# Pooled attention into a snake MLP on one core: k of the first batch summed and turned by TensorE, its rest and half of the next k elsewhere

## The chip, the cores and the metric

The kernel runs on one core of a Trainium2 chip. The metric is the device time of one execution in microseconds; a number of executions gives a median. A profile of one execution shows each engine's instructions: TensorE (PE, with its weight loads as PEld), VectorE (DVE), ScalarE (ACT), GpSimd (POOL) and SyncE (SP), which issues most transfers.

## What is computed

q, k and v have 8 batches, 8 heads, 576 tokens and 64 channels, all float32.

```python
k_p = k.reshape(B, H, Sp, 8, D).mean(axis=3)      # 72 pooled keys
v_p = v.reshape(B, H, Sp, 8, D).mean(axis=3)
attn = softmax(scale * q @ k_p.T)                 # (q x 72) for each head
x = (attn @ v_p), heads side by side              # 4608 x 512
h = x @ w_in                                      # 512 -> 2048
g = h + sin(alpha * h)**2 / alpha
out = g @ w_out                                   # 2048 -> 512
```

## The kernel before

The large products use Strassen's scheme with seven products for eight. One loop, `hidden(u, extra)`, makes h and g for 512 tokens at a time (nine times, `NU`), in 28 slots: slot 7J + k makes product k of group J, in the order 1, 5, 6, 2, 7, 3, 4, and each product is four matmuls of 128x128 by 128x256 on line 734. The attention of the next batch is threaded into these slots. `carry(u)` lists, slot by slot, what else is emitted there: `at(slot, function, arguments)`. Every engine executes its instructions strictly in the order of emission, so this list is the order of each queue: that of SP, which issues transfers, as well as those of the computing engines. An instruction waits only for the data and buffers that it needs, but all behind it on its engine waits too. The results go through a bridge in HBM (`store_g`, `load_g`) to `outputs()`, which makes the last product (line 1034).

Batch 0 has no earlier loop to hide in: `first_batch()` writes its order out by hand. Its q is loaded two heads at a time with four tokens in a row (`load_q_heads`); the last 64 tokens of each head are "rest" (`load_q_rest`, kept in a part of the w_in buffer `A[3]` that is not in use yet). Its v lies in rows of four tokens too (`load_v_rows`), and TensorE adds the rows: in `sum_v_rows` a constant matrix `twos` (128 rows, 64 columns, ones where a column's two rows meet) is one operand and each of the four tokens the other; `eights` (64 rows, a column for 8 rows) does the same for the rest. Its k is loaded two heads at a time by `load_k_twice` into 72 partitions, one for each pooled key, eight tokens in a row; VectorE (pairs 0 and 1) or GpSimd (pairs 2 and 3) adds them in three steps (lines 146 and 148), the last of which writes the sum twice, side by side. `k_head(hp)` has TensorE transpose this (line 337), and ScalarE copies the result into `kb2`, so that each head's pooled k stands in both halves of the partitions. Then for each pair of heads `hp`: `q_head` transposes q (line 348), `products_head` multiplies (line 369), `soft_head` subtracts the maximum (VectorE, lines 375 and 377) and takes the exponential (ScalarE, 379), `norm_head` divides by the sum (lines 385 to 391), `a_head` transposes (419, 425), and `values` multiplies by v (506, 508) and writes x into a "home" buffer. `warm(n, i)` issues n matmuls of the identity matrix whose result nothing reads (line 830).

Batch 1 (the second) comes next: `load_k(1, e)` loads half of its heads (e = 0 or 1) into a "kvin" buffer on 96 partitions, of which there are two, and `pool_rows` has GpSimd add the tokens in three steps (line 117). `k_t` in slot 4 transposes the sums. `pairs_q` reorders its q on ScalarE, `q_t` transposes q, `two_scores` multiplies, `exp` and `norm` (GpSimd, line 328) follow, `turn` transposes 32x32 blocks on VectorE, `move` issues 16 transfers (line 462), and `all_values` in slot 25 multiplies by v (535, 548). `load_v(1, ...)` uses a kvin buffer again and has GpSimd add.

`load_w_in_part(J)` loads the part of w_in for group J, in four transfers; `combine_w_in(J, steps)` makes Strassen's sums of it (line 605) on VectorE or GpSimd. `sums_of_x(u, n)` makes those of x on VectorE (line 707). `score(4)` and `rest_q` treat the rest of q of batch 0. `root()` computes constants from alpha.

Of the kernel before, what the change touches and what calls it, by code (L numbers as in the profile page):

```python
# [14 lines left out]
AX = mybir.AxisListType.X  # L15
AF = mybir.ActivationFunctionType
OP = mybir.AluOpType
PSUM = bass.MemoryType.PSUM

P = 128  # L20
POOL = 8
# [19 lines left out]
class Kernel:  # L41
# [58 lines left out]
        return (qm[:, 0:n].rearrange("p (h t d) -> p h t d", h=self.H, t=4),  # L100
                qm[:64, n:].rearrange("p (h d) -> p h d", h=self.H))

    def load_k(self, b, e):

        Sp, D, NP = self.Sp, self.D, self.NP
        m = Sp // 3
        t = self.kvp.tile([P, 2048], F32, name="kvin")[:NP * m, 0:3 * POOL * D]
        self.nc.sync.dma_start(out=t, in_=self.k[b, NP * e:NP * e + NP].rearrange("h (p x) d -> (h p) (x d)", x=3 * POOL))
        if b not in self.kp:
            self.kp[b] = self.ap.tile([NP * m, 3, 2, D], F32, name="kp")  # L110
        self.pool_rows(t.rearrange("p (j x) -> p j x", j=3), self.kp[b][:, :, e, :])

    def pool_rows(self, t, out):

# [23 lines left out]
        nc.gpsimd.tensor_tensor(out=vz[:], in0=x[:, 0:D].unsqueeze(1).to_broadcast([P, H // 2, D]),  # L138
                                in1=self.mask[:].unsqueeze(2).to_broadcast([P, H // 2, D]), op=OP.mult)

    def load_k_twice(self, i, eng, t):

        Sp, D = self.Sp, self.D
        self.nc.sync.dma_start(out=t, in_=self.k[0, 2 * i:2 * i + 2].rearrange("h (p t) d -> p h (t d)", t=POOL))
        for w in (4 * D, 2 * D):
            eng.tensor_tensor(out=t[:, :, 0:w], in0=t[:, :, 0:w], in1=t[:, :, w:2 * w], op=OP.add)
        both = lambda x: x.unsqueeze(2).to_broadcast([Sp, 2, 2, D])
        eng.tensor_tensor(out=self.k2[:, 2 * i:2 * i + 2], in0=both(t[:, :, 0:D]), in1=both(t[:, :, D:2 * D]), op=OP.add)

    def load_v_rows(self, b, main, rest):  # L150

# [61 lines left out]
    def attention(self, b):  # L213

        nc, D, H, Sp, NP, S = self.nc, self.D, self.H, self.Sp, self.NP, self.S
# [114 lines left out]
        def new_a():  # L330
            self.aM = self.ap.tile([P, 4, 736], F32, name="aM")

        def k_head(hp):

            ps = self.psum([P, 2, Sp], 7 if hp % 2 else 0)
            for e in range(2):
                nc.tensor.transpose(ps[:, e, :], self.k2[:, 2 * hp + e].rearrange("p u d -> p (u d)"), self.ident[:Sp, :Sp])
            nc.scalar.copy(out=self.kb2[:, 2 * hp:2 * hp + 2], in_=ps)

        def q_head(hp):  # L340
# [184 lines left out]
        def all_values():  # L525
# [24 lines left out]
            for hp in hps:  # L550
                to_x(ps[hp].rearrange("p (t j) -> p j t", t=4), hp, 0, 512)
            to_x(rest, slice(0, 4), 512, 64)

        return SimpleNamespace(**{f.__name__: f for f in (k_t, q_t, products, score, two_scores, two_shifts, exp, norm, new_a, turn, move, values, values_rest, all_values,
                                                          k_head, q_head, rest_q, products_head, soft_head, norm_head, norm_rest, a_head, a_rest)})

# [260 lines left out]
    def first_batch(self):  # L819

        nc = self.nc
        self.att = [self.attention(b) for b in range(self.B)]
        A = self.att[0]

        far = [self.home(i, [P, 2, 2, POOL * self.D]) for i in (1, 2)]
        h = [self.hp.tile([P, 4 * POOL * self.D], F32, name="h") for _ in range(2)]
        self.load_alpha(self.hp.tile([P, P], F32, name="s", bufs=1)[:])
        one = self.sm.tile([P, 1], F32, name="one")
        nc.scalar.activation(out=one[:], in_=self.ident[:, 0:1], func=AF.Exp)
        warm = lambda n, i: [nc.tensor.matmul(self.psum([P, P], i), self.ident[:], self.ident[:], start=True, stop=True) for _ in range(n)]  # L830
        warm(3, 3)
        self.turn_alpha()
        tr = self.new_tr()
        nc.gpsimd.memset(tr[:, 2048:], 0.0)
        self.a0 = tr[:, 0:2048].rearrange("p (t j s k) -> p t j s k", t=4, j=4, s=2)
        self.z0 = tr[:, 2048:2560].rearrange("p (t hp x k) -> p t hp x k", t=4, hp=4, x=4)
        n, m = self.H * self.Sp, 2 * self.DM
        self.kb2 = h[1][:, 0:n].rearrange("p (h k) -> p h k", h=self.H)
        self.k2 = h[1][:self.Sp, n:n + m].rearrange("p (h u d) -> p h u d", h=self.H, u=2)
        self.a4 = self.last[:64, 0:512].rearrange("p (j s k) -> p j s k", j=4, s=2)  # L840
        self.z4 = self.last[:64, 512:640].rearrange("p (hp x k) -> p hp x k", hp=4, x=4)
        nc.gpsimd.memset(self.z4, 0.0)
        self.new_q(0)
        for hp in range(4):
            self.load_k_twice(hp, nc.vector if hp < 2 else nc.gpsimd, far[hp // 2][:self.Sp, hp % 2])
            self.load_q_heads(0, 2 * hp, 2 * hp + 2)
        self.load_v_rows(0, h[0][:], self.tp.tile([P, self.DM], F32, name="p5")[:])
        self.load_w_in()
        self.load_w_in_part(0)
        self.q_rest = self.A[3][:64, 0, 512:1024].rearrange("p (h d) -> p h d", h=self.H)  # L850
        A.new_a()
        warm(4, 3)
        A.q_head(0)
        warm(2, 4)
        A.k_head(0)
        for hp in range(4):
            A.products_head(hp)
            if hp < 3:
                warm(2, 1 + (hp + 1) % 2)
                A.q_head(hp + 1)  # L860
                A.k_head(hp + 1)
            A.soft_head(hp)
            if hp == 3:
                self.sum_v_rest(0, 0)
            if hp:
                A.norm_head(hp - 1, nc.vector if hp == 1 else nc.gpsimd)
        self.load_q_rest(0, self.q_rest)
        self.load_q(1)
        for e in range(2):
            self.load_k(1, e)  # L870
        self.load_w_in_part(1)
        A.norm_head(3, nc.vector)
        self.sum_v_rows(0, 0, 2)
        A.a_head(0, (1, 7, 0))
        self.sum_v_rows(0, 1, 2)
        A.values((0, 1), (4, 1))
        self.combine_w_in(0, (0, 1))
        A.a_head(1, (5, 6, 2))
        self.combine_w_in(0, (2, 3), nc.gpsimd)
        self.root()  # L880
        self.sums_of_x(0, 0)

    def carry(self, u):

        x = defaultdict(list)
        at = lambda slot, f, *a: x[slot].append(lambda: f(*a))
        last = self.B - 1
        b = u + 1
        if u == 0:
            A0, A = self.att[:2]  # L890
            at(1, A0.values, (2, 3), (2, 7))
            at(1, self.sums_of_x, 0, 1)
            at(1, self.sums_of_x, 0, 2)
            at(1, self.sums_of_x, 0, 3)
            at(2, self.load_w_in_part, 2)
            at(2, self.load_w_in_part, 3)
            at(2, A0.rest_q)
            at(3, A0.score, 4)
            at(2, self.pairs_q, 1, range(5))
            at(4, self.combine_w_in, 1, (0, 1, 2, 3), self.nc.gpsimd)  # L900
            at(4, A.q_t, 0, self.nc.vector.tensor_copy)
            at(4, A.q_t, 1, self.nc.vector.tensor_copy)
            at(4, A.k_t)
            at(7, self.load_v, 1, 0)
            at(7, self.load_v, 1, 1)
            for i in range(2):
                at((5, 10)[i], A.two_scores, i)
            at(11, A.two_shifts)
            for i in range(2, 5):
                at(5 + i, A.q_t, i)  # L910
            at(9, A0.exp, 4)
            for i in range(4):
                at((9, 9, 15, 15)[i], A.exp, i)
                at((10, 10, 16, 16)[i], A.norm, i)
                at((13, 13, 17, 17)[i], A.turn, i)
            at(8, self.combine_w_in, 2, (0, 1, 2, 3), self.nc.gpsimd)
            at(10, self.combine_w_in, 3, (0, 1, 2, 3), self.nc.gpsimd)
            at(20, A0.norm_rest)
            at(23, A0.a_rest)
            at(24, lambda: A0.values_rest((5, 6, 7, (self.turn + 1) % 5)))  # L920
            for r in (32, 96):
                at(3, self.nc.gpsimd.memset, self.aM[r:r + 32, :, 704:736], 0.0)
            at(17, A.move, 0)
            at(17, A.move, 1)
            at(25, A.all_values)
            at(9, self.load_q, 2)
            at(14, self.load_q, 3)
            for e in range(2):
                at(16, self.load_k, 2, e)
            at(26, self.att[2].k_t)  # L930
            turn = 23
        else:
            at(0, self.sums_of_x, u, 2)
            at(0, self.sums_of_x, u, 3)
        if 0 < u < last:
            A = self.att[b]
# [341 lines left out]
```

## Time and profile before

| | us |
|---|---|
| five runs, median | 925.91 |
| lowest, highest | 922.28, 928.20 |
| the profiled execution, its time | 927.38 |
| the profiled execution, its span | 925.5 |

The span is the time from the first to the last recorded instruction; what lies around it is 1.9 us. A line of the timeline gives the start, the busy time, the engine, the line of the kernel, the operation, and output <- input with partitions x elements; "x32" is the number of instruction records in it, and "[0.37 <-ACT h L338]" is the idle time of the engine ahead of it and what ended it. TensorE's records count a float32 product twice (a `products_head` of 16 matmuls is x32), a transpose once. In a list of waits the columns are: who waited for whom, the total, the number of times, the longest, all in us. In a table by stretch each row gives from:to, the length, then busy us and instructions of PE, PEld, DVE, ACT and POOL, the granted TensorE clock, the busy share of the 16 transfer engines and what they moved in GB/s.

### The profile page before, as it was taken

What the parts mean: (1) busy time and instruction counts of PE and PEld (TensorE: products, weight loads), DVE (VectorE), ACT (ScalarE), POOL (GpSimd) and SP (SyncE); (2) the same over time, 40 slices, a digit from 0 to 9 for tenths busy, and PEclk for the clock granted to TensorE, in tenths of its full rate; (3) what the DMA queues carried; (4) which work ended last, traced back from release to release, by engine and by line L of the source; (5) the groups of instructions that cost most, each with busy time, mean ns of one, the idle gap of its engine ahead of it and who ended that gap; (6) DMA issues with size and microseconds to landing.
All of it is one profiled execution on the core that took longest, in us unless ns stands there. A gap on an engine that the chain in (4) does not pass through costs nothing.

```text
span 925.5 us, 17725 instructions
## 1 busy us (share of the span) xinstructions
PE 903.8 (98%) x7009; PEld 818.0 (88%) x7009; DVE 668.6 (72%) x1007; ACT 436.7 (47%) x995; POOL 163.7 (18%) x155
## 2 busy tenths in 40 slices
PE   7998999999999999999999999999999999999997
PEld 6686888887888888888888899999999999999997
DVE  7665666745657466673466989988888888988894
ACT  4595686864867658676786631111111211112111
POOL 4684250522505225040000000000000000000000
PEclk9999999999999999999999999999999999999999
DMA  9975756766557646636526237161526353433401
GB/s 240 240 220 166 191 154 182 219 177 185 150 175 229 180 131 173 173 118 217 199 92 226 87 120 226 32 222 36 188 69 171 87 167 91 148 110 114 144 14 39
DMA packets 134130, 141.12 MB, mean 152 GB/s; under 512 B 49808, under 2 KB 102048, under 8 KB 134048
## 3 DMA queue, kind: packets, MB, share of 16 engines
q1 hardware_dynamic: 132976, 138.81, 52.0%
q10 hardware_dynamic: 1072, 1.19, 0.4%
q8 instruction: 55, 0.90, 0.4%
q14 instruction: 27, 0.22, 0.1%
HBM read 75.37 MB, written 47.19 MB: 132 GB/s over the span
## 4 chain that ended last, share of the span: by engine, by line
PE 86%; DMA 5%; DVE 2%; POOL 2%; SPq 2%; ACT 1%; issue 1%; POOLq 0%; DVEq 0%; ACTq 0%
PE PS L1034 41%; PE PS L734 40%; PE PS L271 2%; PE PS L535 2%; DMA kvin<-in_v_dram 1%; DMA q<-in_q_dram 1%; DVE sm L326 1%; DMA a<-in_moe_w_in_dram 1%; PE PS L548 1%; POOL as L605 1%; SPq L462 1%; SPq L599 1%; DVE h L713 1%; DMA home<-in_k_dram 1%; POOL ex L328 1%
## 5 line engine op out<-in xcount | busy, mean ns | idle before, releaser
L734 PE MATMUL PS<-home,a 128*128 128x256 f32 x1152 | 266.0, 382 | 5.1 <-DVE h L713 4.2
L734 PEld LDWEIGHTS PS<-home,a 128*128 128x128 f32 x1152 | 216.6, 190 | 44.2 <-DVE h L713 7.5
L734 PE MATMUL PS<-home,as 128*128 128x256 f32 x864 | 201.1, 382 | 1.0 <-DVE home L707 1.0
L734 PEld LDWEIGHTS PS<-home,as 128*128 128x128 f32 x864 | 163.2, 191 | 24.4 <-DVE home L707 2.0
L1034 PE MATMUL PS<-s,wb 128*128 128x144 f32 x896 | 119.3, 286 | 0.4 <-ACT PS L1147 0.4
L1034 PEld LDWEIGHTS PS<-s,wb 128*128 128x128 f32 x896 | 113.7, 190 | 0.7 <-ACT PS L1147 0.6
L713 DVE TENSOR_TENSOR h<-PS,p 128x512 f32<-128x512 f32 x72 | 49.1, 684 | 89.3 <-PE PS L734 55.8
L747 ACT ACTIVATE s<-s,c 128x256 f32<-128x256 f32 (+1 forms) x216 | 110.0, 572 | 0.0
L117 POOL TENSOR_TENSOR kvin<-kvin 96x768 f32<-96x768 f32 (+3 forms) x42 | 70.0, 1667 | 203.5 <-DMA kvin<-in_v_dram 185.2
L740 ACT ACTIVATE s<-h,al 128x256 f32<-128x256 f32 x144 | 65.1, 500 | 63.0 <-DVE h L713 62.1
L1147 ACT COPY PS<-PS 128x144 f32<-128x144 f32 x56 | 14.7, 263 | 146.0 <-PE PS L1034 144.6
L740 ACT ACTIVATE s<-PS,al 128x256 f32<-128x256 f32 x144 | 60.1, 468 | 29.6 <-PE PS L734 21.2
L1034 PE MATMUL PS<-r,wb 128*128 128x144 f32 x512 | 73.2, 286 | 0.0
L1034 PE MATMUL PS<-s,a 128*128 128x144 f32 x512 | 73.2, 286 | 0.0
L801 DVE TENSOR_TENSOR h<-PS,s 128x512 f32<-128x512 f32 x36 | 24.7, 685 | 60.1 <-ACT s L747 60.1
L1034 PEld LDWEIGHTS PS<-r,wb 128*128 128x128 f32 x512 | 67.1, 190 | 0.1
L1034 PEld LDWEIGHTS PS<-s,a 128*128 128x128 f32 x512 | 67.0, 190 | 0.0
L1166 ACT COPY PS<-PS 128x144 f32<-128x144 f32 x56 | 14.7, 263 | 88.2 <-PE PS L1034 88.2
L1034 PE MATMUL PS<-s,we 128*128 128x144 f32 x384 | 54.9, 286 | 0.0
L1034 PE MATMUL PS<-x,wb 128*128 128x144 f32 x384 | 54.9, 286 | 0.0
L1034 PEld LDWEIGHTS PS<-s,we 128*128 128x128 f32 x384 | 50.4, 190 | 0.1
L1034 PEld LDWEIGHTS PS<-x,wb 128*128 128x128 f32 x384 | 50.3, 190 | 0.0
(178 smaller groups left out, 1188.5 us busy)
## 6 DMA issues: line engine op xcount, KB each, us to landing
g_bridge<-h SPq DMA_DIRECT2D x72, 512.0 KB
r<-g_bridge SPq DMA_DIRECT2D x31, 1152.0 KB
out_dram<-o SPq DMA_DIRECT2D x128, 72.0 KB
kvin<-in_k_dram SPq DMA_DIRECT2D x14, 576.0 KB
q<-in_q_dram SPq DMA_DIRECT2D x7, 1024.0 KB
kvin<-in_v_dram SPq DMA_DIRECT2D x14, 512.0 KB
aM<-tr SPq DMA_DIRECT2D x56, 92.0 KB
aM<-tr SPq DMA_DIRECT2D x56, 88.0 KB
```

Source lines behind the costliest of these rows:

```text
L117: self.nc.gpsimd.tensor_tensor(out=t[..., 0:w] if w > D else out, in0=t[..., 0:w], in1=t[..., w:2 * w], op=OP.add)
L271: nc.tensor.matmul(ps[e][r0 + r:r0 + r + q.shape[-1], h, :], q[s], kb[s, hp, :], start=True, stop=True)
L326: nc.vector.tensor_reduce(out=sm, in_=E(i, Sp + 1), axis=AX, op=OP.add)
L535: nc.tensor.matmul(o[r:r + 64], w, x, start=start and i < 2, stop=False, skip_group_check=True)
L713: add = lambda o, x, y: nc.vector.tensor_tensor(out=o, in0=x, in1=y, op=OP.add)
L734: nc.tensor.matmul(ps[:, jj, :], self.A[p][:, kk, f * P:(f + 1) * P], x[:, kk, :], start=(start and jj == 0 and kk == 0), stop=(kk == 1), ...
L740: nc.scalar.activation(out=G.s[:, i, jj, j, :], in_=src[:, jj], func=AF.Sin, scale=self.al[:, f:f + 1])
L747: nc.scalar.activation(out=x, in_=x, func=AF.Square, scale=self.c[:, f:f + 1])
L801: add = lambda o, x, y: self.nc.vector.tensor_tensor(out=o, in0=x, in1=y, op=OP.add)
L1034: nc.tensor.matmul(out, W[:, J // 2, J % 2, :], A[:, J, :], start=(start and J == 0), stop=(J == self.NJ - 1), skip_group_check=True)
L1147: nc.scalar.copy(out=x1[:, 0, :], in_=x0[:, 1, :])
L1166: nc.scalar.copy(out=x1[:, 1, :], in_=x1[:, 0, :])
```

## The change

The k of batch 0 is loaded in the form of q and v: rows of four tokens on 128 partitions, two heads a transfer, and the last 64 tokens of all heads in one transfer, which goes to ScalarE's queue. `load_k_twice` goes. `k_last` has TensorE sum the rest with `eights` for all eight heads, and `k_head` adds the four tokens of the main part with `twos`; as k is the stationary operand, the sums come out turned, and each product is made twice (u), for the two halves of the partitions. Both write into one PSUM bank for the even pairs and one for the odd ones (`k_slots`). Six fillers ahead of `q_head` and two ahead of the first `k_head` go; `k_head` is emitted one pair ahead. `norm_head(0)` moves from VectorE to GpSimd. `load_k(1, e)` and `load_w_in_part(1)` are emitted at the end of `first_batch`, behind w_in's sums on GpSimd; the second half's sum is one VectorE reduction in slot 3 (`half_k`). In the first loop `rest_q` moves from slot 2 to slot 1, `score(4)` from 3 to 2, and two `sums_of_x` from 1 to 2.

```diff
-    def load_k(self, b, e):
+    def load_k(self, b, e, later=False):
...
-        self.pool_rows(t.rearrange("p (j x) -> p j x", j=3), self.kp[b][:, :, e, :])
+        t, out = t.rearrange("p (j x) -> p j x", j=3), self.kp[b][:, :, e, :]
+        if later:
+            return lambda: self.nc.vector.tensor_reduce(out=out, in_=t.rearrange("p j (t d) -> p j d t", t=POOL), axis=AX, op=OP.add)
+        self.pool_rows(t, out)
...
-    def load_k_twice(self, i, eng, t):
...
+    def load_k_rows(self, main, rest):
+        self.k_rows = main.rearrange("p (h t d) -> p h t d", h=self.H, t=4), rest.rearrange("p (h d) -> p h d", h=self.H)
+        self.nc.scalar.dma_start(out=self.k_rows[1], in_=self.k[0, :, 4 * P:, :].rearrange("h p d -> p h d"))
+
+    def load_k_heads(self, h0, h1):
+        self.nc.sync.dma_start(out=self.k_rows[0][:, h0:h1].rearrange("p h t d -> p h (t d)"),
+                               in_=self.k[0, h0:h1, 0:4 * P, :].rearrange("h (p t) d -> p h (t d)", t=4))
...
+        def k_slots(hp):
+            return self.psum([P, 4, Sp], 7 if hp % 2 else 0)[:, 2 * (hp // 2):2 * (hp // 2) + 2]
+
+        def k_last():
+            for hp in range(4):
+                ps = k_slots(hp)
+                for e in range(2):
+                    for u in range(2):
+                        nc.tensor.matmul(ps[64 * u:64 * u + 64, e, 64:Sp], self.k_rows[1][:, 2 * hp + e], self.eights[:, 0:Sp - 64],
+                                         start=(hp < 2 and e == 0), stop=True, skip_group_check=True)
+
         def k_head(hp):
-            ps = self.psum([P, 2, Sp], 7 if hp % 2 else 0)
+            ps = k_slots(hp)
             for e in range(2):
-                nc.tensor.transpose(ps[:, e, :], self.k2[:, 2 * hp + e].rearrange("p u d -> p (u d)"), self.ident[:Sp, :Sp])
+                for t in range(4):
+                    for u in range(2):
+                        nc.tensor.matmul(ps[64 * u:64 * u + 64, e, 0:64], self.k_rows[0][:, 2 * hp + e, t], self.twos[:],
+                                         start=False, stop=(t == 3), skip_group_check=True)
             nc.scalar.copy(out=self.kb2[:, 2 * hp:2 * hp + 2], in_=ps)
...
         for hp in range(4):
-            self.load_k_twice(hp, nc.vector if hp < 2 else nc.gpsimd, far[hp // 2][:self.Sp, hp % 2])
+            self.load_k_heads(2 * hp, 2 * hp + 2)
             self.load_q_heads(0, 2 * hp, 2 * hp + 2)
...
         warm(4, 3)
+        A.k_last()
+        A.k_head(0)
         A.q_head(0)
-        warm(2, 4)
-        A.k_head(0)
+        A.k_head(1)
         for hp in range(4):
             A.products_head(hp)
             if hp < 3:
-                warm(2, 1 + (hp + 1) % 2)
                 A.q_head(hp + 1)
-                A.k_head(hp + 1)
+            if hp < 2:
+                A.k_head(hp + 2)
             A.soft_head(hp)
             if hp == 3:
                 self.sum_v_rest(0, 0)
             if hp:
-                A.norm_head(hp - 1, nc.vector if hp == 1 else nc.gpsimd)
+                A.norm_head(hp - 1, nc.gpsimd)
         self.load_q_rest(0, self.q_rest)
         self.load_q(1)
-        for e in range(2):
-            self.load_k(1, e)
-        self.load_w_in_part(1)
         A.norm_head(3, nc.vector)
...
         self.combine_w_in(0, (2, 3), nc.gpsimd)
         self.root()
         self.sums_of_x(0, 0)
+        self.load_k(1, 0)
+        self.half_k = self.load_k(1, 1, True)
+        self.load_w_in_part(1)
...
             at(1, A0.values, (2, 3), (2, 7))
             at(1, self.sums_of_x, 0, 1)
-            at(1, self.sums_of_x, 0, 2)
-            at(1, self.sums_of_x, 0, 3)
+            at(1, A0.rest_q)
+            at(2, A0.score, 4)
+            at(2, self.sums_of_x, 0, 2)
+            at(2, self.sums_of_x, 0, 3)
             at(2, self.load_w_in_part, 2)
             at(2, self.load_w_in_part, 3)
-            at(2, A0.rest_q)
-            at(3, A0.score, 4)
+            at(3, self.half_k)
             at(2, self.pairs_q, 1, range(5))
```

More of the change, by code (lines that the diff above doesn't have):

```diff
@@ L139, in load_v @@
                                 in1=self.mask[:].unsqueeze(2).to_broadcast([P, H // 2, D]), op=OP.mult)
-    def load_k_twice(self, i, eng, t):
[L143 to L148, printed above, removed]
+    def load_k_rows(self, main, rest):
[4 more added lines that the diff above has]
+                               in_=self.k[0, h0:h1, 0:4 * P, :].rearrange("h (p t) d -> p h (t d)", t=4))
     def load_v_rows(self, b, main, rest):
@@ L554, in attention @@
         return SimpleNamespace(**{f.__name__: f for f in (k_t, q_t, products, score, two_scores, two_shifts, exp, norm, new_a, turn, move, values, values_rest, all_values,
-                                                          k_head, q_head, rest_q, products_head, soft_head, norm_head, norm_rest, a_head, a_rest)})
+                                                          k_last, k_head, q_head, rest_q, products_head, soft_head, norm_head, norm_rest, a_head, a_rest)})
     def load_alpha(self, rows):
@@ L823, in first_batch @@
         A = self.att[0]
-        far = [self.home(i, [P, 2, 2, POOL * self.D]) for i in (1, 2)]
+        far = [self.home(i, [P, 4 * POOL * self.D]) for i in (1, 2)]
         h = [self.hp.tile([P, 4 * POOL * self.D], F32, name="h") for _ in range(2)]
         self.load_alpha(self.hp.tile([P, P], F32, name="s", bufs=1)[:])
+        self.load_k_rows(far[0][:], far[1][:64, 0:self.DM])
         one = self.sm.tile([P, 1], F32, name="one")
@@ L836, in first_batch @@
         self.z0 = tr[:, 2048:2560].rearrange("p (t hp x k) -> p t hp x k", t=4, hp=4, x=4)
-        n, m = self.H * self.Sp, 2 * self.DM
-        self.kb2 = h[1][:, 0:n].rearrange("p (h k) -> p h k", h=self.H)
-        self.k2 = h[1][:self.Sp, n:n + m].rearrange("p (h u d) -> p h u d", h=self.H, u=2)
+        self.kb2 = h[1][:, 0:self.H * self.Sp].rearrange("p (h k) -> p h k", h=self.H)
         self.a4 = self.last[:64, 0:512].rearrange("p (j s k) -> p j s k", j=4, s=2)
```

## The prediction

> **What bounds the kernel now.** I read the first page, then the chain of waits in order of time for the first 92 us, then busy time by stretch, then single instructions. On the page the engine rows and the chain's shares say that TensorE sets the time nearly everywhere:
>
> ```profile
> PE 903.8 (98%) x7009; PEld 818.0 (88%) x7009; DVE 668.6 (72%) x1007; ACT 436.7 (47%) x995; POOL 163.7 (18%) x155
> PE 86%; DMA 5%; DVE 2%; POOL 2%; SPq 2%; ACT 1%; issue 1%; POOLq 0%; DVEq 0%; ACTq 0%
> ```
>
> The change touches only the start, and the shares other than PE's lie there. The chain in order of time (start, us, what):
>
> ```profile
> 1.70 5.31 DMA home<-in_k_dram
> ...
> 16.17 10.95 DMA q<-in_q_dram
> 27.14 9.47 DMA a<-in_moe_w_in_dram
> 36.63 12.81 DMA kvin<-in_v_dram
> 49.48 0.09 issue
> 49.57 2.37 POOL kvin L117
> ...
> 70.53 2.75 POOL ex L328 x2
> ...
> 84.23 2.10 DMA aM<-tr
> ```
>
> So up to 49.5 us the chain is one line of loads: k and q of batch one, v, w_in, q and k of batch two, the rest of w_in, v of batch two. Then GpSimd works without a pause (v's sums, w_in's sums, the normalising of batch two) to 73.3 us; VectorE turns the result, SP moves it in 16 transfers, and TensorE, which has run ahead, takes it at 86.4 us. From about 91 us on the 56 us periods repeat, bound by TensorE. Nothing that the change does reaches them, except that all shift together. Busy time by stretch, of which I use the last two numbers, the transfer engines' busy share and GB/s:
>
> ```profile
> 0.00:5.00 5.00, 3.31 (x14) 3.03 (x15) 1.67 (x8) 1.66 (x3) 2.29 (x10) 1.00 0.57 167
> 5.00:10.00 5.00, 3.90 (x67) 3.54 (x70) 3.70 (x7) 1.62 (x4) 0.02 (x1) 1.00 1.02 228
> 10.00:15.00 5.00, 3.54 (x80) 2.81 (x73) 4.41 (x7) 2.13 (x4) 4.75 (x5) 1.00 1.11 244
> 15.00:20.00 5.00, 3.92 (x71) 3.02 (x70) 4.90 (x9) 2.33 (x6) 2.29 (x4) 1.00 1.12 319
> 20.00:25.00 5.00, 5.00 (x46) 3.06 (x45) 3.79 (x9) 3.14 (x8) 1.75 (x2) 1.00 1.17 250
> ```
>
> The engines are full, yet they move 228 to 244 GB/s while k and q of batch one land, and 319 while v and w_in do, which lie in rows of 1 KB on all 128 partitions.
>
> **The change part by part.** The sum is made against the profiled execution, 927.38 us (span 925.5 and 1.9 around it); the median of the runs shown is 925.91, 1.47 lower.
>
> *Loads.* k of batch one moves the same bytes. Before: four transfers to 72 partitions in rows of 2 KB. After: four in rows of 1 KB on 128 partitions, the form of v_rows, plus one of 128 KB in rows of 256 B on ACT's queue. SP's order stays: k of batch two and w_in's second part move down together, and nothing else that SP issues stands between. Up to 15 us the chip moves 5 x (167 + 228 + 244) KB = 3.2 MB. At v's 319 GB/s and with 2.0 us before the first data that ends at 12.0 us, a gain of 3.0. At the 250 GB/s of the next stretch, where q of batch two moves in q's own form beside other shapes, it ends at 14.8, a gain of 0.2. I take 1.9: nearer to v, since k then has v's form, less something for the 256 B rows. As the line of loads has no hole up to v of batch two, v lands that much earlier: 49.5 becomes 47.6.
>
> The Trainium skill ("DMA: Bandwidth & Descriptors", the section on why a DMA increments its semaphore by 16) states that a transfer is split over the largest number up to 16 that divides its slowest dimension; for 72 partitions that is 12 engines, for 128 all 16. The low GB/s agrees; no view here counts the engines. By the rule alone (an estimate), 16 in place of 12 engines for k's 1.18 MB at 228 GB/s would give about 1.3 us.
>
> *Removed from VectorE and GpSimd.* VectorE loses two k sums of 1.14 + 0.42 us and, as the normalising of pair 0 goes to GpSimd, 2.29 us (two L391, 13.07). GpSimd loses 2.07 + 0.72 and 2.41 + 0.72, and 3.34 + 0.59 of batch two's second k half; it gains the 2 L391, 1.30 to 1.75 us by its own rows. That k half becomes one VectorE reduction of 1536 elements: by the L294 rows (288 elements 0.46 us, 864 elements 1.01, so about 1 ns an element) some 1.7 us. It stands in slot 3, ahead of the copies of q and k that slots 4 and 5 need. The 128 KB issue costs ACT about 0.7 us, as its like for v does SP (L153, 0.73), under ACT's first table load; ACT's next task that matters is at 6.2 us.
>
> *TensorE's head.* Rows count a float32 product twice. Removed: four k_head of 0.29 to 0.34 and eight fillers, 0.61 + 3 x 0.71, in all 4.0 us. Added: four k_head of 32 rows, stationary 128x64, moving 64, and k_last of 32 short rows. Nothing like it runs now. Bounds from both sides:
>
> ```profile
> 7.12 0.73 PE L369 MATMUL PS<-h,q 64*64 64x72 f32 x32 [0.37 <-ACT h L338]
> 17.85 1.09 PE L174 MATMUL PS<-h,twos 128*64 128x128 f32 x16
> ```
>
> 32 rows cost 0.73 us by the first (smaller stationary) and 2.2 by the second (same stationary, twice the columns). I take 1.5, between, as the row lies between in size; k_last 0.7. Rolled forward with 0.6 per q_head, 0.73 per products, and the copies 0.6 and 0.28: with the first rows in at 4.6 k_last ends at 5.3, then come the two k_head and q_head before the products of pair 0 at 8.9, which end at 9.6, against 7.85 now. After that a pair of heads costs 0.73 + 0.6 + 1.5 = 2.8 us, and the products of pairs 1 to 3 end at 12.4, 15.2 and 17.5, against 10.5, 14.35 and 17.57. Now pairs 2 and 3 wait for GpSimd's sums (0.78 and 0.70 before L337); those waits go, and what is late next is TensorE itself. Then a_head waits for GpSimd's normalising of pair 1, 17.75 + 1.75 = 19.5, against 18.96. The head comes out about even: 0.3 us later, from 1.6 earlier (k_head 0.73) to 2.5 later (2.2).
>
> *Slots 0 to 5.* TensorE loses three waits there now:
>
> ```profile
> PE PS L734 <- DVE home L707: 1.0, 1, 1.0
> PE PS L734 <- POOL a L605: 0.8, 1, 0.8
> PE PS L233 <- POOL kp L117: 0.4, 1, 0.4
> ```
>
> The second goes, as w_in's two GpSimd sums now stand ahead of k of batch two, where GpSimd waits 7.7 us for that k. The first is filled by score(4) (0.72), moved ahead of product 6. The third stays, now for VectorE's 1.7 us reduction, which has the sums of x and score's shifts in front of it; behind it queue the q and k copies, and product 7 waits for them: about 0.8 lost. Net 0.8 + 0.7 - 0.8 = 0.7 earlier, so with the head 0.4 earlier at slot 5 (41.2 now), and so on to slot 15.
>
> *The joint.* GpSimd's last normalising starts at 70.53, when GpSimd is free; what it needs from TensorE's side was there at 69.1, a slack of 1.4. After: free at 68.6, ready at 68.7. TensorE's long wait,
>
> ```profile
> PE PS L734 <- DVE h L713: 2.9, 1, 2.9
> ```
>
> ends with VectorE behind that normalising, so TensorE being early cannot go past it. All that follows shifts by 1.7, rounded down for the second pair (ready at 70.3 now, 69.9 after). 927.38 - 1.7 = 925.7; at the level of the median, **924.2**.
>
> *The removed fillers.* The first products on the identity take 0.26 us each (2.07 for 8 rows at 3.5 us), those at 6.0 us 0.15 (0.61 for 4), both at a granted clock of 1.00. So TensorE starts slow and quickens with work. The Trainium skill ("TensorE: Matmul & The Clock Gate", Part 1) says that an idle window of about 3.4 us halves the clock, and (Part 4) that transposes don't count as work, which speaks against taking fillers out. No gap of this head is over 0.8 us, and k_head now is products where it was transposes; by the rule the clock stays.
>
> **The rivals.**
> - *Both sides give all they have.* Loads at 319 GB/s (3.0), and then v's own rows, which land at 116 to 171 GB/s between 40 and 50 us, no longer mixed with w_in's, by over 2 us more; k_head at 0.73 (head 1.6 earlier), and all of the 2.0 us that TensorE idles in slots 0 to 4 gone: 3.6 earlier plus the 1.4 of slack is 5.0: 920.9. For it: the engines are full the whole time, so each packet saved counts. Against: the VectorE reduction.
> - *The loads gain nothing.* 256 B rows and a second queue eat the gain. Then v lands at 49.5, GpSimd's line starts as now, and whatever TensorE gains ends in a longer wait before 75.4: 925.9. For it: q in its own form at 250 GB/s.
> - *Slower: k_head becomes the head's bound.* It stands in TensorE's order between the products of one pair and the next. Up to 1.9 us each the slack covers it. At 2.2 the head is 3.1 us late, less 0.7 and 1.4: 1.0 slower. At the speed of the first rows, twice as long (4.4 us each), pair 3's products end 11.3 us later, at 28.9; less about 2.0 caught up in slots 0 to 5 and the 1.4 of slack that is about 8 us: 934. For it: the fillers go. Against: the gaps are short.
>
> **How the numbers follow.** A measurement of this kernel can tell about 0.5%, 4.6 us. Chances: forecast 0.40 (its own range 922.5 to 926), no gain from the loads 0.23, both together "same" 0.63; all gains 0.27, "faster"; k_head bound 0.10, "slower". The range 918 to 929.5 reaches beyond the 920.9 of the second case by the runs' scatter (922.28 to 928.2) and on the other side to the mild form of the slow case with the same scatter.
>
> **What would show it.** Right: 300 GB/s or more between 5 and 15 us; GpSimd's v sums begin near 47.6; the wait for L713 stays at 2 to 3 us; the periods after 91 us keep 56 us. The steps fail singly if k_head's 32 rows take over 1.9 us, if the first product of slot 0 starts outside 23 to 27 us (24.89 now), or if TensorE waits for the reduction by more than 1 us. The prediction is wrong if v does not land earlier, or if the normalising at 70.5 starts later than 70.5.

## The result and the profile after

The changed kernel takes 929.19 us (median of 29 runs, 926.74 to 931.64) against 924.63 for the kernel before (55 runs, 921.70 to 932.68): ratio 1.0044, interval 1.0033 to 1.0055. It is slower by 4 to 5 us where I forecast 1.7 less. The profiled execution of after took 927.68 (span 925.9). That of before, 927.38, was one of its slower ones (its repeat below has a span of 920.4 beside 925.5), so the two profiles side by side show less than the medians do.

The loads did what the prediction asked of them. Stretches of the trace after (from:to, length, then busy us and instructions of PE, PEld, DVE, ACT, POOL, the granted clock, the transfer engines' share, GB/s):

```profile
5.00:10.00 5.00, 5.00 (x71) 4.55 (x70) 0.00 (x0) 0.28 (x1) 0.00 (x0) 1.00 1.12 324
10.00:15.00 5.00, 5.00 (x141) 4.15 (x140) 2.08 (x3) 2.32 (x6) 0.00 (x0) 1.00 1.10 329
15.00:20.00 5.00, 4.00 (x116) 3.20 (x118) 4.45 (x9) 2.71 (x5) 1.39 (x3) 1.00 0.56 144
```

324 and 329 GB/s where 228 and 244 were moved. In the third row the transfers have run dry: SP stands still for 6.1 us with q of batch two, until TensorE's last `q_head` has read what lies in that place, and asks for it at 17.86, where before did at 15.59. What came of it stands in the list of GpSimd's waits and in the longest pieces of the chain (start, us, what):

```profile
POOL ex L332 <- ACT PS L792: 5.2, 1, 5.2
POOL kvin L120 <- DMA kvin<-in_v_dram: 4.9, 1, 4.9
```

```profile
5.56 1.81 PE PS L347 x32
7.37 1.90 PE PS L356 x32
17.86 5.69 DMA q<-in_q_dram
25.04 9.73 DMA a<-in_moe_w_in_dram
34.79 9.38 DMA kvin<-in_v_dram
44.30 2.37 POOL kvin L120
53.73 2.32 POOL a L625
61.80 8.38 PE PS L754 x38
75.14 1.78 DVE h L733 x3
84.60 2.08 DMA aM<-tr
...
540.71 4.31 DMA g_bridge<-h
547.01 2.48 DVE x L1010
```

The first two rows are TensorE's new work on k: up to 17.86 us the chain is now TensorE, where it was loads, and the loads of batch two start behind it. v still lands at 44.3 instead of 49.5, 5.2 earlier, and GpSimd then waits 5.2 us ahead of the last normalising (line 328, now 332): TensorE is in the chain again at 61.8 and the normalising starts at 70.89, not at 68.6. The last two rows are new: near 541 us the chain goes through a store to the bridge. Now TensorE's timeline (start, busy us, operation, idle time and what ended it) and its two waits in slots 2 to 4:

```profile
5.49 1.88 PE L347 MATMUL PS<-eights,home 64*64 64x8 f32 x32
7.30 1.97 PE L356 MATMUL PS<-twos,home 128*64 128x64 f32 x32
9.21 1.09 PE L368 MATMUL PS<-ident,q 128*128 128x128 f32 x4
10.23 1.15 PE L356 MATMUL PS<-twos,home 128*64 128x64 f32 x32
11.31 0.73 PE L389 MATMUL PS<-h,q 64*64 64x72 f32 x32
...
21.01 1.09 PE L439 MATMUL PS<-ident,tr 128*128 128x128 f32 x8 [0.40 <-POOL tr L411]
...
26.93 1.89 PE L754 MATMUL PS<-home,a 128*128 128x256 f32 x8
```

```profile
PE PS L237 <- DVE kp L113: 1.4, 1, 1.4
PE PS L754 <- DVE home L727: 1.3, 1, 1.3
```

The first products start at 11.31 (7.12 before), a_head at 21.01 (18.96), slot 0 at 26.93 (24.89). Far behind the change's reach, ScalarE's timeline at the joint of the two loops has a wait that before lacks. Of after, then of before:

```profile
542.48 0.26 ACT L1168 COPY PS<-PS 128x144 f32<-128x144 f32 x1 [3.59 <-PE PS L1055]
545.16 0.70 ACT L1094 COPY ca<-PS 128x288 f32<-128x288 f32 x2 [2.42 <-DMA g_bridge<-h]
```

```profile
544.15 0.26 ACT L1147 COPY PS<-PS 128x144 f32<-128x144 f32 x1 [3.59 <-PE PS L1034]
544.39 0.70 ACT L1073 COPY ca<-PS 128x288 f32<-128x288 f32 x2
```

### The profile page after: what moved, and what is told of

It is laid out like the page before. It is cut to its first block, busy times and chain, and to the rows that moved or that the text cites. A ratio compares the mean times of both kernels' runs of the same rounds, so it can differ in the third digit from the quotient of the medians.

```text
span 925.9 us, 17985 instructions
## 1 busy us (share of the span) xinstructions
PE 907.2 (98%) x7145; PEld 821.2 (89%) x7145; DVE 666.0 (72%) x1000; ACT 436.3 (47%) x995; POOL 156.3 (17%) x148
## 4 chain that ended last, share of the span: by engine, by line
PE 86%; DVE 5%; DMA 4%; POOL 1%; ACT 1%; issue 1%; SPq 1%; ACTq 0%; DVEq 0%; POOLq 0%
PE PS L754 41%; PE PS L1055 39%; PE PS L275 2%; PE PS L555 2%; DVE sm L330 1%; DMA a<-in_moe_w_in_dram 1%; DMA kvin<-in_v_dram 1%; PE PS L568 1%; SPq L482 1%; DVE h L733 1%; DMA q<-in_q_dram 1%; PE PS L356 1%; DVE x L1010 1%; DMA g_bridge<-h 0%; PE PS L851 0%
## 5 line engine op out<-in xcount | busy, mean ns | idle before, releaser
L120 POOL TENSOR_TENSOR kvin<-kvin 96x768 f32<-96x768 f32 (+3 forms) x40 | 66.5, 1662 | 199.4 <-DMA kvin<-in_v_dram 189.3
```

The source lines that it names most:

```text
L120: self.nc.gpsimd.tensor_tensor(out=t[..., 0:w] if w > D else out, in0=t[..., 0:w], in1=t[..., w:2 * w], op=OP.add)
```

## The experiments

The theory after seeing this: three things cost, TensorE's longer head, the VectorE reduction and the wait for the bridge, and they outweigh the loads. The rival: the rows' TensorE work alone is the loss. Below, "g0" and "g2" are the last additions of the first and third group of the first loop (VectorE), by which a profile's start can be compared with another's.

**Both kernels again.**

> The kernel before, unchanged, for a second profile. The two profiled executions differ by 0.4 us in span while the medians differ by 4.6 us (924.6 and 929.2), so one or both profiles are not typical. Theory HEAD (the whole loss lies ahead of 91 us, in TensorE's own k sums): the first values of batch two end at 88 to 90 us here, not at 91.2 as in the first profile, and the later marks are equal. Theory LATE (the loss lies after 91 us, in stalls that come and go, as the 2.3 us stall of TensorE at 220 us): they end at 91 again, and the 2.3 us stall at 220 us is absent or shorter. Time 924 to 926, ratio to itself 1.000 within 0.2%.

> The changed kernel, unchanged, for a second profile. HEAD: the first values of batch two end at 91.5 us or later, and after it nothing differs from before. LATE: 91.5 again, and beyond it stalls that the kernel before does not have (the joint of the two loops, 540 to 556 us, or a stall near 220 us), 2 us or more in sum. Time 928 to 930, ratio 1.003 to 1.0055.

Before 923.97 (ratio 0.999, 0.997 to 1.001), after 928.86 (1.0047, 1.0027 to 1.0066). In this pair of profiles the loss stands in two places, so each theory holds in part: g0 is 4.0 later (50.62, 54.61), g2 4.15, the first output 6.46. Before, then after:

```profile
79.55 1.22 DVE L801 TENSOR_TENSOR h<-h,s 128x1024 f32<-128x1024 f32 x1
550.77 1.88 SPq L1057 DMA_DIRECT2D out_dram<-o  x4
```

```profile
83.70 1.22 DVE L821 TENSOR_TENSOR h<-h,s 128x1024 f32<-128x1024 f32 x1
557.23 1.89 SPq L1078 DMA_DIRECT2D out_dram<-o  x4
```

This profile of before is the fastest of its twelve runs, so the pair shows 1 to 2 us more than the medians do. v's sums start at 46.55 in it and at 45.46 in this one of after: at 49.57 the line of loads had been late in the profile that I predicted from (46.5 to 48.5 in the five other profiles that load batch one's k as before).

**Each half of the change alone.** The first has only batch one's k in rows of four (loads, `k_last`, `k_head`, order of the head); the second has only what happens to batch two's k and the slots.

> Only k of batch one is changed (rows of four tokens, k_last and k_head on TensorE, fillers out); k of batch two, w_in's second part, rest_q, score(4), the sums of x and norm_head(0) stay as before. HEAD: TensorE's k sums (1.1 to 1.9 us each, first products at 11.4 in place of 7.1) cost the same here: 928 to 930, ratio 1.003 or more. SLOTS (the loss comes from the 2.8 us VectorE reduction in slot 3 and what waits behind it): 924 to 926, ratio below 1.002. LATE: 928 to 930 if the stalls follow the number of TensorE instructions (136 more records), with the head of this profile no longer than 91.2 us.

> k of batch one as before (VectorE and GpSimd sum it, fillers in); only k of batch two and w_in's second part are moved behind w_in's sums, the second half is summed by the VectorE reduction in slot 3, and rest_q, score(4) and the sums of x take their new slots. HEAD: same or up to 1 us faster, 923.5 to 925, ratio 0.999 to 1.001. SLOTS: slower by 2 to 4 us, ratio 1.002 to 1.0045, with TensorE waiting over 1 us ahead of k_t and GpSimd's normalising at 70.5 us no earlier. LATE: as before, 924 to 926.

The second half's core, in the kernel before:

```diff
-        for e in range(2):
-            self.load_k(1, e)
-        self.load_w_in_part(1)
...
+        self.load_k(1, 0)
+        self.half_k = self.load_k(1, 1, True)
+        self.load_w_in_part(1)
...
+            at(3, self.half_k)
```

The rows alone: 931.66 (1.0070, 1.0043 to 1.0097), g2 6.2 later than in the repeat of before and 2.3 more lost at the joint. The slots alone: 925.27 (1.0003, 0.998 to 1.0027), with the same wait of 1.4 for the reduction and nothing lost at the joint. So the loss comes with the rows and what they bring along; the other half as a whole is about neutral.

**The joint: places of two buffers.** The pool of the two h buffers gives places in the order of first use. In the kernel before, `load_k_twice` writes `k2`, in h[1], first; with it gone, h[0] (v's rows) is first, and the two places are swapped. By the addresses in the built programs the last group's h then lies on bytes 84,864 to 93,056 of each partition, and `ca` of `outputs()` begins at 91,520: it must wait until that h has been stored to the bridge. One instruction that touches one buffer early swaps them, in either kernel:

```diff
+        nc.gpsimd.memset(h[1][:, 2047:2048], 0.0)     # after: places as in before
+        nc.gpsimd.memset(h[0][:, 2047:2048], 0.0)     # before: places as in after
```

> The changed kernel with one more instruction: GpSimd writes zero to one unused column of the second h buffer before v is loaded, so that the two h buffers get the places that they have in the kernel before (places are given in the order of first use: in the kernel before k's sums touch the second one first, in the changed one v's load touches the first one first, and all 36 later tiles follow). Theory JOINT: in the changed kernel the last group's h lies under the first output block 'ca', so ScalarE waits 2.4 us at 542.6 us for the last store to the bridge, and TensorE loses 2.1 to 2.3 us between 540 and 556 us; here that loss is gone: the time from the last group's final add to the first output is 15.1 us, not 17.3, and the time 926.5 to 927, 2.2 us below the changed kernel. Rival: the wait comes from the number of transfers (one more, so other semaphores); then nothing changes, 929.

> The kernel before with the mirror edit: GpSimd writes one unused column of the first h buffer first, so the h buffers swap places as in the changed kernel; nothing else. JOINT: slower by 2.2 us, ratio 1.002 to 1.003, and the profile shows ScalarE's wait of 2 to 2.5 us ahead of its first copy to 'ca' and 17.3 us from the last group's final add to the first output in place of 15.1. Rival (number of transfers): no change, 15.1 us.

The kernel before with after's places: 927.63 (1.0027, 1.0011 to 1.0043), with the wait in its list for ScalarE:

```profile
ACT ca L1074 <- DMA g_bridge<-h: 2.3, 1, 2.3
```

From the last group's addition to the first output it takes 15.15 to 15.17 us with before's places and 17.2 to 17.5 with after's, whichever kernel it is. But the other direction first missed: after with before's places lost nothing at the joint (15.16), and its median was still 928.71 (1.0045, 1.0032 to 1.0059, six runs). A second set follows after the next experiment.

**The reduction.** The kernel after with before's places, and the second k half summed by GpSimd in three steps, as before:

```diff
-        if later:
-            return lambda: self.nc.vector.tensor_reduce(out=out, ...)
         self.pool_rows(t, out)
```

> e5 with the second half of batch two's k summed by GpSimd (three steps, line of the first half) in place of VectorE's reduction, which takes 2.80 us at 38.2 us in the changed kernel's profile and makes TensorE wait 1.36 us ahead of k_t. Theory REDUCTION: that wait goes, slots 5 to 17 come 1.0 to 1.4 us earlier than in e5, and as the joint at 71 us hangs on TensorE's and ScalarE's side there now, the time is 1.0 to 1.4 us lower, 925.2 to 926. Rival HEAD (the whole delay of slots 5 to 17 is made before slot 0): no gain, TensorE waits for GpSimd's sums at k_t instead, 926.5 to 927.5, since GpSimd's 3.9 us of sums now stand ahead of w_in's.

925.20 (1.0013, 1.0001 to 1.0025): TensorE's wait for k is gone, and with the same head as the repeat of after (slot 0 at 28.37 and 28.34) g2 is 1.3 earlier. Then a set of four, to price each alone on top of after:

> The kernel after with one edit: the second half of batch two's k is summed by GpSimd as before; the h buffers stay in after's places. Theory (the reduction with what queues behind it costs some 2 to 3 us, and the places another 2 on top): 926 to 927.3, 2 to 3 us below after in the same set and 1 to 2.5 above the same kernel with the other places (925.2). Rival (the places cost nothing in most executions, as the median of after with the other places suggested): 925 to 925.5.

> The kernel after with the h buffers in the places of before, a second time, since its first median rested on six executions. Theory (the joint costs about 2 us in every execution): 1.5 to 2.5 us below after in this set, near 927. Rival (what is gained at the joint is not there at the level of the medians): within 1 us of after.

> The kernel after, as the measure for this set: 928.5 to 929.5, 4 to 5 us above before, by either theory.

After 929.74 (1.0055, 1.0033 to 1.0076); with GpSimd's sums 926.57 (1.0017, 1.0001 to 1.0033); with before's places 926.58 (1.0019, 1.0002 to 1.0036). Each undoes some 3 us. For the places the two sets disagree (1.0045 with six runs, 1.0019 with twelve); I go by the larger, which agrees with the 1.0027 of the swap in before. The profiles of both sets show something that can hide the gain: VectorE's addition ahead of the reduction took 1.75 us in place of 0.68, the wait grew to 2.8 and 2.4, and then the granted clock fell. How often that happens in the runs without a profile is not known. The second of the two, TensorE's timeline and its stretches:

```profile
42.66 0.71 PE L237 MATMUL PS<-ident,kp 96*128 96x96 f32 x3 [2.39 <-DVE kp L113]
43.17 3.28 PE L754 MATMUL PS<-home,a 128*128 128x256 f32 x8
```

```profile
41.00:42.00 1.00, 0.00 (x0) 0.00 (x0) 1.00 (x1) 1.00 (x3) 0.00 (x0) 1.00 1.00 211
42.00:43.00 1.00, 0.34 (x2) 0.37 (x3) 1.00 (x2) 0.51 (x2) 0.00 (x0) 0.75 1.06 229
43.00:44.00 1.00, 1.00 (x5) 0.90 (x4) 1.00 (x3) 0.00 (x0) 0.00 (x0) 0.50 0.87 166
44.00:45.00 1.00, 1.00 (x4) 0.74 (x3) 0.16 (x1) 0.00 (x0) 0.00 (x0) 0.50 0.34 104
45.00:46.00 1.00, 1.00 (x4) 0.82 (x3) 0.00 (x0) 0.00 (x0) 0.33 (x1) 0.54 0.26 96
```

A product of 1.89 us takes 3.28 at half the clock. So the reduction costs about 1.3 us where the clock holds (wait of 1.4), and 3.2 (g2 at 85.65 instead of 82.40) where it doesn't. The Trainium skill ("TensorE: Matmul & The Clock Gate", Part 1) says that the gate closes after an idle window of about 3.4 us. Here a wait of 2.4 was enough.

**The slots' moves with GpSimd's sums.** The kernel before with only the moves, without the reduction, in two sets:

> The kernel before with only the moves of batch two's k, rest_q, score and the sums of x, its second half still summed by GpSimd; no change of batch one's k, so TensorE's head and the h buffers' places are those of before. Theory (of the change's parts the VectorE reduction is what costs in the slots, the moves themselves win the 0.7 us of the removed waits): median 923 to 924, 1 to 2 us below the variant with the reduction (925.27), no wait for the k sum over 0.5 us. Rival (GpSimd reaches the second k half too late and v's sums start later, the loads of v land later as k is asked for later): 925 to 926.

> The kernel before with only the slots' moves, the second k half on GpSimd, a second time. Theory (the moves win what the removed waits were worth): 0.5 to 2 us below before, ratio 0.998 to 0.9995. Rival (the first result was scatter): ratio 1.000.

923.37 (0.9984, 0.997 to 0.9999) and 923.39 (0.9990, 0.9973 to 1.0006), beside 925.27 with the reduction. This is the best median measured, 1.3 us below before; only the first of the two intervals excludes 1. My expectation of the wait was a miss: TensorE still waits 1.7 and 1.9 us for k, now from GpSimd. Where the gain arises is not shown: in these two profiles g2 comes at 80.14 and 81.82, later than the 79.55 in the repeat of before.

**TensorE's head.** Its first rows run slow: 32 rows of `k_head` take 1.97 us at 7.3 and 1.15 at 10.2. More fillers on the kernel after with before's places:

```diff
-        warm(4, 3)
+        warm(8, 3)
```

> e5 with eight fillers in place of four ahead of k_last. In the changed kernel TensorE's rows go from slow to quick only at about 10 us (first q_head 4 rows in 1.09 us at 9.2 us, second k_head 1.15 us at 10.2), in the kernel before at 6.0 to 6.7 us. Theory CLOCK: the many small k_last products with 8 columns do not count as work, so the clock stays low; with 2 us more of full 128-column products before them the switch comes by 7.5 us, the first k_head takes 1.1 to 1.2 us in place of 2.0, k_last under 1.2 in place of 1.9, and the first products start at 10.5 to 11.5, no later than the 11.3 to 13.3 now: 0.5 to 1.5 us gained, 925.5 to 926.5. Rival WAIT (k_last waits for the 256 B rows that land at 5.5 to 7 us, and only the number of rows counts): the fillers just take 2 us more in front, first products at 12.5 to 14, 927 to 928.5.

927.47 (1.0034, 1.0018 to 1.0051), between the two medians of the same kernel without them, so a gain can't be told. The fillers quickened TensorE (`k_last` 1.10, the first `k_head` 1.15), but this profile has a pause of 1.7 at 14.0, put down to a w_in transfer that the next rows do not read, and a half clock after a wait of only 1.27 at 32.2. Then, with GpSimd's sums as well, `k_last` split so that 8 rows stand ahead of each `k_head`, and that with the fillers:

```diff
-        def k_last():
-            for hp in range(4):
+        def k_last(hps):
+            for hp in hps:
...
         def k_head(hp):
+            k_last((hp,))
```

> The kernel after with the h buffers in their places of before, the second half of batch two's k summed by GpSimd, and now k_last split: eight rows ahead of each k_head instead of 32 rows ahead of the first. Theory (TensorE's head is what is late, and k_last stands in it as serial work ahead of the first products): the first products start about 1.4 us earlier than with all of k_last in front (11.3 in the profile of after), a_head about 1 us earlier, the median 924 to 925. Rival (the head is paced by k_head itself, or by GpSimd's normalising): products of pair 0 earlier, a_head unmoved, median 925.2 as without the split.

> The previous kernel with eight instead of four of the second kind of fillers ahead of the head. Theory (TensorE runs slow until about 10 us because k_last's products of eight columns do not quicken it): the fillers quicken it by 7 to 8 us, k_head's 32 rows take 1.15 us from the first, products of pair 0 start near 10.5, median 0.5 to 1 us below the kernel without them. Rival (fillers cost what they win): median the same within 0.5 us.

925.52 (1.0006, 0.9994 to 1.0017) and 925.80 (1.0007, 0.999 to 1.0024), against 925.20 (1.0013) without the split in another set: by the ratios some 0.6 us less, within the intervals, and no difference between the two. TensorE's timeline of the first, without the added fillers, then of the second:

```profile
7.80 0.60 PE L346 MATMUL PS<-eights,home 64*64 64x8 f32 x8 [2.22 <-DMA home<-in_k_dram]
8.33 1.97 PE L356 MATMUL PS<-twos,home 128*64 128x64 f32 x32
...
13.72 0.89 PE L389 MATMUL PS<-h,q 64*64 64x72 f32 x32
```

```profile
3.56 3.78 PE L852 MATMUL PS<-ident 128*128 128x128 f32 x16
7.27 0.56 PE L346 MATMUL PS<-eights,home 64*64 64x8 f32 x8
7.76 1.15 PE L356 MATMUL PS<-twos,home 128*64 128x64 f32 x32
...
10.84 0.73 PE L389 MATMUL PS<-h,q 64*64 64x72 f32 x32
```

With the fillers all rows of `k_head` take 1.15 and the first products start at 10.84, 2.9 earlier than at 13.72 (0.5 of that because the rest of k, whose 256 B rows landed at 7.8 there, kept TensorE waiting; the other 2.4 by quicker rows). Slot 0 comes at 27.88 in place of 30.03, g2 at 81.42 in place of 83.91. The medians do not show this, and why is open. But even so slot 0 is 3.1 later than in the repeat of before (24.80): the work itself stands ahead of the first products. Last, a hybrid: the loads of after, but VectorE and GpSimd add the four tokens and write the sum twice; TensorE only adds two rows and turns, one product of 128x128 by 64 columns a head:

```diff
+        eng.tensor_tensor(out=x[:, :, 0:2 * D], in0=x[:, :, 0:2 * D], in1=x[:, :, 2 * D:4 * D], op=OP.add)
+        eng.tensor_tensor(out=self.k2[:, 2 * hp:2 * hp + 2], in0=both(x[:, :, 0:D]), in1=both(x[:, :, D:2 * D]), op=OP.add)
...
+                nc.tensor.matmul(ps[:, e, 0:64], self.k2[:, 2 * hp + e].rearrange("p u d -> p (u d)"), self.twos[:], ...)
```

> A hybrid: batch one's k is loaded in rows of four tokens as after, but VectorE (pairs 0, 1) and GpSimd (pairs 2, 3) add the four tokens in two instructions and write the sum twice, as before; TensorE only adds two rows and turns, two products a head pair of 128x128 by 64 in place of 16 of 64 columns wide stationary, plus eight short rows for the rest; fillers, order of k_head and places of the h buffers as before; batch two's k half on GpSimd. Theory (loads gain 2 us or more, and the loss was TensorE's head, the reduction and the places): TensorE's head at or before the kernel before, a_head at 18 to 19.5, v's sums near 45, GpSimd's slack grows, median 921.5 to 923.5, below both kernels. Rival (past the head TensorE is what bounds, and it gains nothing from earlier loads): 923.5 to 925, the same as before.

924.90 (1.0009, 0.9989 to 1.0030): my theory's 921.5 to 923.5 missed, the rival holds. Its profile is the fastest of all (span 917.9), but not by its start: its g2, 79.32, is 0.2 earlier than in the repeat of before, and the rest of its lead of 2.5 lies behind, where nothing was changed. TensorE's pauses near 220 and 335 us (1.26 and 1.23 in that repeat) are missing in it. Its twelve runs reach from 919.7 to 933.1; that spread I can't explain. What the hybrid tells is in GpSimd's timeline:

```profile
67.34 2.83 POOL L339 TENSOR_TENSOR ex<-ex,sm 128x576 f32<-128x576 f32 x2 [3.45 <-DVE sm L338]
```

v's sums start at 43.77, 2.8 earlier than in the repeat of before (46.55), slot 0 at 25.66 (24.80), and the last normalising at 67.34 against 67.60. Of 2.8 us of earlier loads 0.3 are left; the rest is GpSimd's new wait of 3.45.

## Why the prediction was wrong

- *The bound.* "All that follows shifts by 1.7" failed. I read from one profile that loads and GpSimd end last up to 73 us. That was so there, with v at 49.6; the repeat has v at 46.6. Once v is earlier, TensorE ends last ahead of that normalising, and a slack of 1.4 was what I had granted it. GpSimd's wait of 5.2 us, in both profiles of after, and the hybrid show it. The normalising starts at 70.89 and 71.81, which was my sign of being wrong ("later than 70.5").
- *"The line of loads has no hole."* It has one now: in all twelve profiles with the new loads SP stands still for 4.7 to 8.4 us ahead of q of batch two, until TensorE's last `q_head` (1.5 in the repeat of before). So the loads themselves hang on TensorE's head. Where the head is latest (slot 0 at 30.03, the split without added fillers), v's sums start at 48.94, in the other eleven between 43.77 and 46.85.
- *Loads.* 300 GB/s or more, and v earlier: right (329 GB/s; v 1.1 to 5.3 earlier by the pairs of profiles, my 1.9 between them). What failed is its worth.
- *TensorE's head, the mis-sized term.* Predicted 0.3 later, measured 2.0 (slot 0 26.93 after 24.89; 3.5 in the repeats). `k_head` at full speed was within its bounds and below my 1.5: 1.15. But the first one took 1.97 (over the 1.9 that I had named as a failure), `k_last` 1.88 (I took 0.7) and the first `q_head` 1.09 (0.6), and `k_last` started at 5.5 behind the fillers, where I had the first rows in at 4.6 (in seven of the nine profiles with this head and four fillers it waited 0.4 to 2.2 us more for the rest of k, 1.3 in the repeat; I had no term for that). The products of pair 0 ended at 12.0 in place of my 9.6. I had written that TensorE starts slow and quickens with work, and then priced these rows at their quick cost. In before it is quick from 6.0 us (6.5 in the repeat), in after from about 10: the products of 8 columns did not quicken it, and four more fillers ahead of them did, by 7.3. They also show that it isn't the main part: with every row quick, slot 0 still comes 3.1 later than in the repeat of before. This is the slower rival's place, at a price of about 2.4 us (ratio 1.0013 with the new loads and head, 0.9987 without, the mean of two sets), not its 8. The rows alone cost more, 6.5 us, or some 4 without the joint; in that profile TensorE's wait for the sums of x is 2.1 (0.8 to 1.3 in the three of after), and half the clock follows it.
- *The reduction.* Predicted 1.7 us and 0.8 lost; it took 2.80 and TensorE waited 1.4, with up to 1.4 more through the clock. I scaled reductions of rows that lie side by side in PSUM to one that steps through SBUF; 1.8 ns an element in place of 1, and which difference makes it slower was not tested. My line of failure ("waits for the reduction by more than 1 us") was crossed.

```profile
38.18 2.80 DVE L113 TENSOR_REDUCE kp<-kvin 96x192 f32<-96x1536 f32 x1
```

- *The slots.* The wait for GpSimd's `a` went, as said. The wait for x's sums was to go and became 1.3. Net over slots 0 to 5: 0.0 instead of 0.7 earlier. TensorE's wait for L713, which was to stay at 2 to 3 us, fell to 1.3, but it is 1.0 in the repeat of before as well.
- *"Nothing that the change does reaches them"* (the 56 us periods and what follows). The periods held; the joint behind them did not. I had put this at nothing. The edit moved no instruction there, it only changed which buffer was used first: 2.1 to 2.4 us in every trace with these places.
- *Sums that do not agree with themselves.* `k_head` at 2.2 us makes the head 2.5 late in one place and 3.1 in another, and TensorE's three waits are 2.2 us together, not 2.0. Neither changes the outcome.

The sum in us, each with an interval of 1.5 or more: the moves −1.2, the rows with TensorE's head +2.4, the reduction +1.5 (ratio 1.0003 less 0.9987) to +3.2, the places +2.5 to +3.2 in medians (nothing in the six runs; 2.1 to 2.4 in traces); in all 5 to 8, where after measures 4.1 to 5.1. That the reduction and the places cost is shown by undoing each alone; the share of the rows is a difference of ratios from two sets. On the variant with both edits undone, putting one of them back cost less (1.0017 and 1.0019 beside 1.0013, across two sets), so the shares may not add; that is left open.

## What to carry to other kernels

Before counting a transfer's gain, price the path that ends next, from more than one profile: a start that is bound by loads in one execution can be bound by TensorE in the next. When an edit removes the first use of a rotating buffer, look where the buffers lie afterwards and who shares their bytes, even hundreds of us away. When loads get faster, look which transfer then waits for its place. A short new wait on TensorE costs more than its length as soon as the clock falls with it.

## What the runs showed of the hardware

The granted clock fell to about half for some 3 us after waits of 2.4 and 2.8 us (after with before's places), 2.1 (the rows alone, and the moves in their second set) and once 1.27 (more fillers), but stayed at 1.00 after 2.9 in the profile of before and 2.1 in that of the slots alone. Short additions of VectorE and GpSimd now and then take 1.1 us more than their like (1.75 for 0.68, 2.35 for 1.27). Both of these stand beside an addition of the other engine: GpSimd's 2.35 at 53.69 in after beside VectorE's 1.22 at 53.68, VectorE's 1.75 at 38.09 beside GpSimd's 1.74 at 37.55; that one holds up the other is not tested. And TensorE pauses by 0.8 to 2.3 us near 220 us in 17 of the 18 profiles and by 0.7 to 1.5 near 335 in 13, with no release that the trace shows (1.77 at 221.5 in after); 16 KB instruction loads stand beside the pauses, which was not tested.
